# A single-token attention-plus-gMLP block on one core: issuing K and V from the first microsecond, with the weights threaded between heads and one epilogue for both rows

## The chip, the cores and the metric

The kernel runs on one core of one Trainium2 chip. The metric is the device time of one launch in microseconds; medians of several executions are given, and the profile comes from one further execution. The span of the profile is 1.7 us shorter than the device time of the same execution (726.7 against 728.44 us before the change).

Ratios are the mean time of one kernel's fast executions over that of the other's in the same rounds, so they are not quite the ratio of the medians that are quoted.

## The reference, cut to what matters

```python
# B=2 rows, D=512; H=32 heads, Sk=8192 cached keys, Dh=128; F=1792; all bf16
xn = layernorm(x)
q = xn @ wq                                   # wq [512, 4096]
p = softmax(q . k_cache * Dh**-0.5)           # k_cache, v_cache [2, 32, 8192, 128]
attn = (p @ v_cache) @ wo                     # wo [4096, 512]
z = gelu(xn @ w_in)                           # w_in [512, 1792]
z1, z2 = halves(z)
mlp = (z1 * (w_sp * layernorm(z2) + b_sp)) @ w_out   # w_sp and b_sp are one number each
return x + attn + mlp
```

K and V are 268 MB, and each byte is used once. Everything else is 11 MB of weights and some small arithmetic.

## The kernel before

For each of the 64 (row, head) pairs the kernel loads K and V (2 MB each), multiplies K by the broadcast q on VectorE, folds the 128 products of every key by halving adds, lets ScalarE take the exponential, and lets TensorE (PE) form the weighted sum of V. In front stands a prologue: layernorm, q for all heads of both rows, and the whole gMLP. Behind each row stands an epilogue.

```python
pro = pro_stack.enter_context(tc.tile_pool(name="pro", bufs=1))
...
nc.scalar.dma_start(x_rows[:], ...)           # all weights: one block on ScalarE's queue
for c in range(NQC):
    nc.scalar.dma_start(wq_sb[...], ...)
... # x_b, w_sp, b_sp, w_in, w_out, wo, also on nc.scalar
... # layernorm with Ln and Exp; q of both rows; the whole gMLP, ending in hT
pro_stack.close()                             # K and V take over the prologue's memory

kpool = ctx.enter_context(tc.tile_pool(name="kpool", bufs=3))
vpool = ctx.enter_context(tc.tile_pool(name="vpool", bufs=3))
for b in range(B):
    for h in range(H):
        kt = kpool.tile([P, J, Dh], BF16, name="kt")
        nc.sync.dma_start(kt[:], A_k_cache[b, h]...)
        vt = vpool.tile([P, J, Dh], BF16, name="vt")
        nc.sync.dma_start(vt[:], A_v_cache[b, h]...)
        nc.vector.tensor_tensor(out=kt[:], in0=kt[:], in1=q_bcast, op=ALU.mult)
        ... # six halving adds on kt, then the last one into s_t
        nc.scalar.activation(out=e_t[:], in_=s_t[:], func=ACT.Exp, ...)
        ... # 64 matmuls of V by e_t into o_ps[:, h]
    ... # this row's epilogue: l_ps, reciprocal, o_sb, 7 hT and 32 wo matmuls, res, store
```

The scheduler was free to move instructions within an engine's order.

The softmax here doesn't subtract the row's maximum and nothing guards it: scores larger than these inputs give would overflow.

Of the kernel before, what the change touches and what calls it, by code (L numbers as in the profile page):

```python
# [7 lines left out]
BF16 = mybir.dt.bfloat16  # L8
# [6 lines left out]
def kernel(  # L15
# [14 lines left out]
    nc = tc.nc  # L30
# [17 lines left out]
    HPC = NQ // Dh  # L48
# [3 lines left out]
    work = ctx.enter_context(tc.tile_pool(name="work", bufs=2))  # L52
    psum_main = ctx.enter_context(tc.tile_pool(name="psum_main", bufs=1, space=bass.MemoryType.PSUM))
# [5 lines left out]

    x_rows = pro.tile([B, D], BF16, name="x_rows")  # L60
    nc.scalar.dma_start(x_rows[:], A_x.flatten_outer_dims())
    wq_sb = pro.tile([P, KD, HD], BF16, name="wq_sb")
    for c in range(NQC):
        nc.scalar.dma_start(  # L64
            wq_sb[:, :, c * NQ:(c + 1) * NQ],
            A_wq[:, c * NQ:(c + 1) * NQ].rearrange("(k p) n -> p k n", p=P),
        )
    x_b = []
    for b in range(B):
        xb = const.tile([1, D], BF16, name=f"x_b{b}")  # L70
        nc.scalar.dma_start(xb[:], A_x[b])  # L71
        x_b.append(xb)
    wsp_sb = pro.tile([P, 1], BF16, name="wsp_sb")
    nc.scalar.dma_start(wsp_sb[:], B_w_sp[0:1, 0:1].to_broadcast((P, 1)))
    bsp_sb = pro.tile([P, 1], BF16, name="bsp_sb")
    nc.scalar.dma_start(
# [3 lines left out]
    nc.scalar.dma_start(w_in_sb[:], B_w_in.rearrange("(k p) f -> p k f", p=P))  # L80
    w_out_sb = const.tile([P, FC, N_OUT], BF16, name="w_out_sb")
    nc.scalar.dma_start(w_out_sb[:], B_w_out.rearrange("(c p) n -> p c n", p=P))
    wo_sb = const.tile([P, H, N_OUT], BF16, name="wo_sb")
    nc.scalar.dma_start(wo_sb[:], A_wo.rearrange("(h p) n -> p h n", p=P))

    ident = const.tile([B, B], F32, name="ident")
    nc.gpsimd.memset(ident[:], 0.0)
    nc.gpsimd.affine_select(
        out=ident[:],
        in_=ident[:],  # L90
        compare_op=ALU.not_equal,
        fill=1.0,
        base=0,
        pattern=[[-1, B]],
        channel_multiplier=1,
    )
    ones_f = const.tile([P, P], F32, name="ones_f")
    nc.gpsimd.memset(ones_f[:], 1.0)
# [20 lines left out]
    eps_b = pro.tile([B, 1], F32, name="eps_b")  # L119
    nc.vector.memset(eps_b[:], EPS)  # L120
    lnv = pro.tile([B, 1], F32, name="lnv")
    nc.scalar.activation(out=lnv[:], in_=var[:], func=ACT.Ln, bias=eps_b[:], scale=1.0)  # L122
    rstd = pro.tile([B, 1], F32, name="rstd")
    nc.scalar.activation(out=rstd[:], in_=lnv[:], func=ACT.Exp, scale=-0.5)  # L124
# [15 lines left out]
    for b in range(B):  # L140
        for k in range(KD):
            nc.vector.tensor_copy(
                out=xn_rep[:, b, k, :], in_=xnT[:, k, b:b + 1].to_broadcast([P, P])
            )

    qbc = []
    for b in range(B):
        qb = const.tile([P, HD], BF16, name=f"qbc{b}")
        for c in range(NQC):
            q_ps = psum_q.tile([P, NQ], F32, name="q_ps")  # L150
            for k in range(KD):
                nc.tensor.matmul(  # L152
                    q_ps[:], lhsT=xn_rep[:, b, k, :], rhs=wq_sb[:, k, c * NQ:(c + 1) * NQ],
                    start=(k == 0), stop=(k == KD - 1),
                )
            nc.scalar.copy(out=qb[:, c * NQ:(c + 1) * NQ], in_=q_ps[:])  # L156
        qbc.append(qb)

    for c in range(NC2):
        for k in range(KD):  # L160
            nc.tensor.matmul(  # L161
                z_ps[:, c, :], lhsT=w_in_sb[:, k, c * P:(c + 1) * P], rhs=xnT[:, k, :],
                start=(k == 0), stop=(k == KD - 1),
            )
    z_sb = pro.tile([P, NC2, B], F32, name="z_sb")
    nc.vector.tensor_copy(out=z_sb[:], in_=z_ps)  # L166
    zsq = pro.tile([P, NC2, B], F32, name="zsq")
    nc.vector.tensor_tensor(out=zsq[:], in0=z_sb[:], in1=z_sb[:], op=ALU.mult)
    zt = pro.tile([P, NC2, B], F32, name="zt")
    nc.vector.tensor_scalar(out=zt[:], in0=zsq[:], scalar1=0.044715, scalar2=1.0,  # L170
                            op0=ALU.mult, op1=ALU.add)
    nc.vector.tensor_tensor(out=zt[:], in0=zt[:], in1=z_sb[:], op=ALU.mult)
    zexp = pro.tile([P, NC2, B], F32, name="zexp")
    nc.scalar.activation(out=zexp[:], in_=zt[:], func=ACT.Exp, scale=-1.5957691216057308)
    zsig = pro.tile([P, NC2, B], F32, name="zsig")
    nc.vector.tensor_single_scalar(out=zsig[:], in_=zexp[:], scalar=1.0, op=ALU.add)
    nc.vector.reciprocal(out=zsig[:], in_=zsig[:])
    zg = pro.tile([P, NC2, B], F32, name="zg")
    nc.vector.tensor_tensor(out=zg[:], in0=z_sb[:], in1=zsig[:], op=ALU.mult)
    stat = pro.tile([P, 2 * B], F32, name="stat")  # L180
    nc.vector.reduce_sum(
        out=stat[:, 0:B], in_=zg[:, FC:NC2, :].rearrange("p c b -> p b c"),
        axis=mybir.AxisListType.X,
    )
    z2sq = pro.tile([P, FC, B], F32, name="z2sq")
    nc.vector.tensor_tensor(out=z2sq[:], in0=zg[:, FC:NC2, :], in1=zg[:, FC:NC2, :], op=ALU.mult)
    nc.vector.reduce_sum(
        out=stat[:, B:2 * B], in_=z2sq[:].rearrange("p c b -> p b c"),
        axis=mybir.AxisListType.X,
    )  # L190
    nc.tensor.matmul(stat_ps, lhsT=ones_f[:], rhs=stat[:], start=True, stop=True)
    zmean = pro.tile([P, B], F32, name="zmean")
    nc.vector.tensor_single_scalar(out=zmean[:], in_=stat_ps[:, 0:B], scalar=1.0 / Fh, op=ALU.mult)
    zmsq = pro.tile([P, B], F32, name="zmsq")
    nc.vector.tensor_tensor(out=zmsq[:], in0=zmean[:], in1=zmean[:], op=ALU.mult)
    zvar = pro.tile([P, B], F32, name="zvar")
    nc.vector.scalar_tensor_tensor(
        out=zvar[:], in0=stat_ps[:, B:2 * B], scalar=1.0 / Fh, in1=zmsq[:],
        op0=ALU.mult, op1=ALU.subtract,
    )  # L200
    eps_p = pro.tile([P, 1], F32, name="eps_p")
    nc.vector.memset(eps_p[:], EPS)
    zln = pro.tile([P, B], F32, name="zln")
    nc.scalar.activation(out=zln[:], in_=zvar[:], func=ACT.Ln, bias=eps_p[:], scale=1.0)
    zrstd = pro.tile([P, B], F32, name="zrstd")
    nc.scalar.activation(out=zrstd[:], in_=zln[:], func=ACT.Exp, scale=-0.5)  # L206
    wsp_f = pro.tile([P, 1], F32, name="wsp_f")
    nc.vector.tensor_copy(out=wsp_f[:], in_=wsp_sb[:])  # L208
    bsp_f = pro.tile([P, 1], F32, name="bsp_f")
    nc.vector.tensor_copy(out=bsp_f[:], in_=bsp_sb[:])  # L210
    a_t = pro.tile([P, B], F32, name="a_t")
    nc.vector.tensor_single_scalar(out=a_t[:], in_=zrstd[:], scalar=wsp_f[:, 0:1], op=ALU.mult)
    c_t = pro.tile([P, B], F32, name="c_t")
    nc.vector.tensor_tensor(out=c_t[:], in0=zmean[:], in1=a_t[:], op=ALU.mult)
    nc.vector.tensor_scalar(out=c_t[:], in0=c_t[:], scalar1=-1.0, scalar2=bsp_f[:, 0:1],
                            op0=ALU.mult, op1=ALU.add)
    g_t = pro.tile([P, FC, B], F32, name="g_t")
    for b in range(B):
        nc.vector.tensor_scalar(
            out=g_t[:, :, b], in0=zg[:, FC:NC2, b], scalar1=a_t[:, b:b + 1],  # L220
            scalar2=c_t[:, b:b + 1], op0=ALU.mult, op1=ALU.add,
        )
    hT = const.tile([P, FC, B], BF16, name="hT")
    nc.vector.tensor_tensor(out=hT[:], in0=zg[:, 0:FC, :], in1=g_t[:], op=ALU.mult)  # L224
    pro_stack.close()

    kpool = ctx.enter_context(tc.tile_pool(name="kpool", bufs=3))
    vpool = ctx.enter_context(tc.tile_pool(name="vpool", bufs=3))
    spool = ctx.enter_context(tc.tile_pool(name="spool", bufs=3))
    l_all = const.tile([P, B * H], F32, name="l_all")  # L230
    o_sb = const.tile([P, B, H], BF16, name="o_sb")

    for b in range(B):
        o_ps = psum_ob.tile([P, H], F32, name="o_ps")
        for h in range(H):
            gh = b * H + h
            kt = kpool.tile([P, J, Dh], BF16, name="kt")
            nc.sync.dma_start(kt[:], A_k_cache[b, h].rearrange("(p j) d -> p j d", p=P))
            vt = vpool.tile([P, J, Dh], BF16, name="vt")
            nc.sync.dma_start(vt[:], A_v_cache[b, h].rearrange("(p j) d -> p j d", p=P))  # L240
# [18 lines left out]
            for j in range(J):  # L259
# [3 lines left out]
                )  # L263
        l_ps = psum_main.tile([P, H], F32, name="l_ps")
        nc.tensor.matmul(l_ps[:], lhsT=ones_f[:], rhs=l_all[:, b * H:(b + 1) * H],  # L265
                         start=True, stop=True)
        lr = work.tile([P, H], F32, name="lr")
        nc.vector.reciprocal(out=lr[:], in_=l_ps[:])  # L268
        nc.vector.tensor_tensor(out=o_sb[:, b, :], in0=o_ps[:], in1=lr[:], op=ALU.mult)  # L269
# [49 lines left out]
```

## Time and profile before

728.31 us median (726.98 to 730.50, 16 executions). The span of the profile divides as follows. A multiply of K marks the start of each head; "stretch" means from the start of the first multiply to the end of the last head's last add.

| part | us | how it is read |
|---|---|---|
| before the first multiply | 52.9 | timeline |
| 64 heads, 10.21 each | 653.4 | timeline: distance of two multiplies |
| the rest of the stretch, 5.1 of it the stall between the rows | 5.3 | stretch of 658.8 less 653.4 |
| from the last add to the end ("tail") | 14.9 | timeline |
| VectorE busy | 644.2 (89%) | the page's first part |
| DMA while it is backlogged | 423 to 430 GB/s | GB/s row below, slices 5 to 19 |

From the page of the kernel before, second part: the span in 40 equal slices, the busy share of VectorE and of the DMA engines in tenths, and the GB/s moved.

```profile
DVE  1129999999999999999988999999999999999992
...
DMA  9949999999999999999997999999999999999910
GB/s 304 310 180 432 426 427 430 423 427 428 428 428 425 428 428 426 426 430 426 413 419 315 401 408 412 407 411 419 404 411 414 425 395 421 398 413 417 411 80 0
```

VectorE is almost idle in the first three slices (one to two tenths busy) and full afterwards, except in the middle. DMA moves weights in the first two slices and is half idle in the third, before K starts. Both are full in the long stretch. VectorE needs 10.21 us per head; DMA needs 9.8 us, since K and V land 4.90 us apart while there is a backlog. A margin of 4% is not much room. The Trainium skill, "DMA: Bandwidth & Descriptors", section "Specifications", puts the fabric's ceiling at 435 GB/s; the trace's 423 to 430 lies just below it.

The timeline of the kernel before, start to first multiply. Columns: start in us, duration in us, engine and line, operation, output<-inputs, count, and in brackets the idle time of the engine and what ended it. ACT is ScalarE, DVE is VectorE, SPq is SyncE's queue of DMA issues.

```profile
16.04 1.28 ACT L122 ACT_TABLE_LOAD   x1 [16.04 <-DMA bsp_sb<-in_B_b_sp_dram]
...
19.17 0.53 DVE L126 TENSOR_SCALAR xn_rows<-x_f,mean,rstd 2x512 f32<-2x512 f32 x1 [2.88 <-ACT rstd L124]
...
38.30 0.19 DVE L166 COPY z_sb<-zst_ps 128x28 f32<-128x28 f32 x1 [16.48 <-PE zst_ps L161]
...
44.85 0.17 DVE L224 TENSOR_TENSOR hT<-zg,g_t 128x14 bf16<-128x14 f32 x1
...
45.15 0.36 SPq L238 DMA_DIRECT2D kt<-in_A_k_cache_dram  x1
...
52.93 4.43 DVE L242 TENSOR_TENSOR kt<-kt,qbc 128x8192 bf16<-128x8192 bf16 x1 [7.91 <-DMA kt<-in_A_k_cache_dram]
```

ScalarE issued the weights until 16.0 us and only then began the layernorm's logarithm, though VectorE had its input ready at 4.25. (The first line names the landing of b_sp, which fell at the same moment; the logarithm does not read it.) The prologue ended with hT at 45.0 us, and K was issued right then: the waits of SyncE's queue (us in total, times, longest) name hT as what it waited for last.

```profile
SPq L238 <- DVE hT L224: 24.2, 1, 24.2
```

K does not need hT as data: it waited for the prologue's memory to come free.

The row boundary of the kernel before, VectorE's part of the timeline:

```profile
382.68 0.36 DVE L268 RECIPROCAL lr<-l_ps 128x32 f32<-128x32 f32 x1 [2.85 <-PE l_ps L265]
...
383.19 4.42 DVE L242 TENSOR_TENSOR kt<-kt,qbc 128x8192 bf16<-128x8192 bf16 x1
...
392.34 0.68 DVE L287 TENSOR_TENSOR res<-out_ps,x_b 1x512 bf16<-1x512 f32 x1 [1.15 <-PE out_ps L281]
...
395.10 4.42 DVE L242 TENSOR_TENSOR kt<-kt,qbc 128x8192 bf16<-128x8192 bf16 x1
...
405.31 4.42 DVE L242 TENSOR_TENSOR kt<-kt,qbc 128x8192 bf16<-128x8192 bf16 x1
```

The last two lines stand the usual 10.21 us apart. VectorE waited 2.85 us for PE's sums and 1.15 us for the first row's output. The multiply of the head before had started at 369.54, so two distances are long here, 13.65 and 11.91 us instead of 10.21, 5.1 us in sum. The tail of the kernel before, PE's part:

```profile
712.22 1.85 PE L260 MATMUL o_ps<-e_t,vt 128*128 128x1 bf16 x64 [8.37 <-ACT e_t L255]
713.93 0.61 PE L265 MATMUL l_ps<-l_all,ones_f 128*128 128x32 f32 x2
715.22 8.58 PE L281 MATMUL out_ps<-wo_sb,o_sb 128*1 128x512 bf16 x32 [0.68 <-DVE o_sb L269]
```

### The profile page before, as it was taken

Reading aid. Unit: us, or ns where it says so; the run is one execution under the profiler, and the core shown is the slowest. Engines: PE = TensorE matmul, PEld = TensorE weight load, DVE = VectorE, ACT = ScalarE, POOL = GpSimd, SP = SyncE. Lnnn points to the kernel's source line nnn. Section 1 sums busy time; section 2 is a strip of 40 time slices with the busy share of each in tenths; the row PEclk is TensorE's granted clock in tenths of the full one; section 3 lists DMA queues with packets and bytes.
Section 4 is the critical chain, followed back from the end, with each engine's and each line's share of the span. In section 5 each row is a group of like instructions: output and inputs, shape, how many; then the busy total and the mean of one; then the engine's idle time right before and its main releaser. Section 6 shows DMA issues by size and latency. Waiting matters only on the chain.

```text
span 726.7 us, 9772 instructions
## 1 busy us (share of the span) xinstructions
PE 159.7 (22%) x4304; PEld 132.0 (18%) x4304; DVE 644.2 (89%) x558; ACT 38.4 (5%) x153; POOL 0.6 (0%) x7
## 2 busy tenths in 40 slices
PE   0831222122211222122217112221122212221126
PEld 0411221111111111011113111111111101111112
DVE  1129999999999999999988999999999999999992
ACT  1520000000000000000000000000000000000000
POOL 0000000000000000000000000000000000000000
PEclk9965555555555555555557555555555555555557
DMA  9949999999999999999997999999999999999910
GB/s 304 310 180 432 426 427 430 423 427 428 428 428 425 428 428 426 426 430 426 413 419 315 401 408 412 407 411 419 404 411 414 425 395 421 398 413 417 411 80 0
DMA packets 28550, 280.21 MB, mean 386 GB/s; under 512 B 2518, under 2 KB 11612, under 8 KB 12124
## 3 DMA queue, kind: packets, MB, share of 16 engines
q1 hardware_dynamic: 18432, 268.44, 88.6%
q10 hardware_dynamic: 10076, 11.15, 4.7%
q8 instruction: 33, 0.54, 0.3%
q14 instruction: 9, 0.07, 0.0%
HBM read 279.58 MB, written 0.00 MB: 385 GB/s over the span
## 4 chain that ended last, share of the span: by engine, by line
DVE 86%; PE 6%; DMA 3%; issue 2%; ACTq 1%; ACT 1%; DVEq 0%; SPq 0%
DVE kt L246 46%; DVE kt L242 37%; DVE s_t L251 3%; PE out_ps L281 2%; DMA kt<-in_A_k_cache_dram 2%; PE q_ps L152 2%; ACTq L64 1%; DMA bsp_sb<-in_B_b_sp_dram 1%; PE o_ps L260 1%; ACTq L71 0%; PE zst_ps L161 0%; DVE res L287 0%; ACT L206 0%; ACT L124 0%; ACT L122 0%
## 5 line engine op out<-in xcount | busy, mean ns | idle before, releaser
L246 DVE TENSOR_TENSOR kt<-kt 128x4096 bf16<-128x4096 bf16 (+5 forms) x384 | 337.0, 878 | 13.1
L242 DVE TENSOR_TENSOR kt<-kt,qbc 128x8192 bf16<-128x8192 bf16 x64 | 282.8, 4419 | 8.1 <-DMA kt<-in_A_k_cache_dram 8.1
L260 PE MATMUL o_ps<-e_t,vt 128*128 128x1 bf16 x4096 | 118.0, 165 | 535.3 <-ACT e_t L255 535.3
L260 PEld LDWEIGHTS <-vt 128*128 128x128 bf16 x4096 | 114.9, 104 | 539.6 <-issue 526.0
L255 ACT ACTIVATE e_t<-s_t 128x64 bf16<-128x64 f32 x64 | 16.5, 258 | 645.8 <-DVE s_t L251 645.8
L251 DVE TENSOR_TENSOR s_t<-kt 128x64 f32<-128x64 bf16 x64 | 19.3, 301 | 6.4
L281 PE MATMUL out_ps<-wo_sb,o_sb 128*1 128x512 bf16 x64 | 17.6, 443 | 1.4 <-DVE o_sb L269 1.4
L152 PE MATMUL q_ps<-wq_sb,xn_rep 128*128 128x512 bf16 x64 | 16.0, 416 | 0.0
L166 DVE COPY z_sb<-zst_ps 128x28 f32<-128x28 f32 x1 | 0.2, 187 | 16.5 <-PE zst_ps L161 16.5
L255 ACT ACTIVATION_READ_ACCUMULATOR e_t<-s_t 128x1 f32 x64 | 12.1, 188 | 0.1
L208 DVE CAST wsp_f<-wsp_sb 128x1 f32<-128x1 bf16 x1 | 0.2, 154 | 11.7 <-DMA wsp_sb<-in_B_w_sp_dram 11.7
L287 DVE TENSOR_TENSOR res<-out_ps,x_b 1x512 bf16<-1x512 f32 x2 | 1.4, 678 | 9.8 <-PE out_ps L281 9.8
L156 ACT CAST qbc<-q_ps 128x512 bf16<-128x512 f32 x16 | 9.4, 587 | 9.4 <-PE q_ps L152 9.4
L152 PEld LDWEIGHTS <-xn_rep 128*128 128x128 bf16 x64 | 6.7, 106 | 8.8 <-issue 2.1
L281 PEld LDWEIGHTS <-o_sb 128*1 128x1 bf16 x64 | 5.9, 94 | 12.3 <-issue 5.0
L275 PE MATMUL out_ps<-w_out_sb,hT 128*1 128x512 bf16 x14 | 4.8, 501 | 4.7 <-DVE hT L224 3.9
L268 DVE RECIPROCAL lr<-l_ps 128x32 f32<-128x32 f32 x2 | 0.7, 358 | 5.7 <-PE l_ps L265 5.7
L136 PE MATMUL zst_ps<-ident,xn_rows 2*128 2x2 f32 x4 | 0.6, 240 | 19.9 <-DVE xn_rows L126 19.9
L136 PEld LDWEIGHTS zst_ps<-ident,xn_rows 2*128 2x128 f32 x4 | 0.5, 209 | 19.8 <-issue 19.8
L126 DVE TENSOR_SCALAR xn_rows<-x_f,mean,rstd 2x512 f32<-2x512 f32 x1 | 0.5, 532 | 2.9 <-ACT rstd L124 2.9
L275 PEld LDWEIGHTS <-hT 128*1 128x1 bf16 x14 | 1.3, 98 | 7.4 <-DVE hT L224 4.0
L122 ACT ACT_TABLE_LOAD x1 | 1.3, 1283 | 16.0 <-DMA bsp_sb<-in_B_b_sp_dram 16.0
(51 smaller groups left out, 20.0 us busy)
## 6 DMA issues: line engine op xcount, KB each, us to landing
kt<-in_A_k_cache_dram SPq DMA_DIRECT2D x64, 2048.0 KB, 10.4
vt<-in_A_v_cache_dram SPq DMA_DIRECT2D x64, 2048.0 KB, 13.4
wq_sb<-in_A_wq_dram ACTq DMA_DIRECT2D x8, 512.0 KB, 7.9
wo_sb<-in_A_wo_dram ACTq DMA_DIRECT2D x1, 4096.0 KB, 21.4
w_in_sb<-in_B_w_in_dram ACTq DMA_DIRECT2D x1, 1792.0 KB, 9.9
w_out_sb<-in_B_w_out_dram ACTq DMA_DIRECT2D x1, 896.0 KB, 11.0
x_b<-in_A_x_dram ACTq DMA_DIRECT2D x2, 1.0 KB
out_dram<-res ACTq DMA_DIRECT2D x2, 1.0 KB
```

Source lines behind the costliest of these rows:

```text
L64: nc.scalar.dma_start(wq_sb[:, :, c * NQ:(c + 1) * NQ], A_wq[:, c * NQ:(c + 1) * NQ].rearrange("(k p) n -> p k n", p=P),)
L122: nc.scalar.activation(out=lnv[:], in_=var[:], func=ACT.Ln, bias=eps_b[:], scale=1.0)
L152: nc.tensor.matmul(q_ps[:], lhsT=xn_rep[:, b, k, :], rhs=wq_sb[:, k, c * NQ:(c + 1) * NQ], start=(k == 0), stop=(k == KD - 1),)
L156: nc.scalar.copy(out=qb[:, c * NQ:(c + 1) * NQ], in_=q_ps[:])
L242: nc.vector.tensor_tensor(out=kt[:], in0=kt[:], in1=q_bcast, op=ALU.mult)
L246: nc.vector.tensor_tensor(out=kt[:, :, 0:hw], in0=kt[:, :, 0:hw], in1=kt[:, :, hw:w], op=ALU.add)
L251: nc.vector.tensor_tensor(out=s_t[:].unsqueeze(2), in0=kt[:, :, 0:1], in1=kt[:, :, 1:2], op=ALU.add)
L255: nc.scalar.activation(out=e_t[:], in_=s_t[:], func=ACT.Exp, scale=SCALE, accum_out=l_all[:, gh:gh + 1],)
L260: nc.tensor.matmul(o_ps[:, h:h + 1], lhsT=vt[:, j, :], rhs=e_t[:, j:j + 1], start=(j == 0), stop=(j == J - 1),)
L275: nc.tensor.matmul(out_ps[:], lhsT=hT[:, c, b:b + 1], rhs=w_out_sb[:, c, :], start=(idx == 0), stop=(idx == n_mm - 1),)
L281: nc.tensor.matmul(out_ps[:], lhsT=o_sb[:, b, h:h + 1], rhs=wo_sb[:, h, :], start=(idx == 0), stop=(idx == n_mm - 1),)
L287: nc.vector.tensor_tensor(out=res[:], in0=out_ps[:], in1=x_b[b][:], op=ALU.add)
```

## The change

The intent: start K and V at once instead of after the prologue, let the prologue's work ride in gaps between heads, and pay for one epilogue instead of two. The diff, cut to its core:

```diff
+    kpool, vpool, spool opened first: K and V have their own memory; V bufs 3 -> 2
+    ctx.enter_context(tc.manual_schedule(engines={DVE, PE, Activation, SP}))  # order as written
-    nc.scalar.dma_start(...)                 # all weights up front
+    nc.sync.dma_start(x_rows[:], ...)        # x, wq chunk 0, then K0, K1, V0, ...
+    issue_wq(0)
+    nc.gpsimd.dma_start(wsp_sb[:], ...)      # the two scalars, from GpSimd
+    nc.gpsimd.dma_start(bsp_sb[:], ...)
-    activation(Ln); activation(Exp, scale=-0.5)
+    activation(Sqrt); vector.reciprocal
+    make_rep(0); make_q(0, 0)                # q for the first four heads only
+    def issue_kv(b, h): ...                  # K runs one head ahead of V in the queue
+    def loads(b, h):                         # weights behind head h's K and V
+        if b == 0 and h % 4 == 1: issue_wq(h // 4 + 1)
+        if b == 1: w_in at h == 2; w_out at h == 10; one of 8 chunks of wo at h == 12, 14, ... 26
+    def small(b, h):                         # small work behind head h
+        if b == 0 and h % 4 == 2: make_q(0, h // 4 + 1)
+        if b == 0 and h == 12: make_rep(1)
+        if b == 0 and h >= 24: make_q(1, h - 24)
+        if b == 1 and 5 <= h <= 9: next(gm)  # the gMLP in five pieces
-    two epilogues with [1, 512] outputs
+    # one epilogue: 7 hT matmuls, l_ps for both rows, reciprocal, o_sb, 32 wo matmuls, res
```

## The prediction

> **What bounds the kernel now.** VectorE: 97% busy from 60 to 380 and from 400 to 700 us (windowed table). In the timeline a multiply starts every 10.21 us, so 64 heads are 653.4 us of the 726.7 us span. The rest:
> - the first multiply starts at 52.93 us; no K is issued before 45.15, which waited for hT, the prologue's last result (queue waits);
> - between the rows a stall of 5.1 us (15.35 us between the K issues at 379.86 and 395.21);
> - 15.0 us from the last add (711.72) to the end.
>
> DMA is nearly as loaded. While backlogged, transfers of K or V land 4.90 us apart (428 GB/s), so 9.8 us per head. Weights are 11.15 MB; wq chunks (0.5 MB) land 1.51 us apart.
>
> **What changes.** K and V start right behind x and the first wq chunk; the other weights ride between heads on the same queue; q is made by chunks; the gMLP is cut into pieces behind heads 5 to 9 of row 1; one epilogue serves both rows; V has two buffers, not three.
>
> Terms, in us:
> 1. Start: -42.2. q for the first heads is ready near 9.4 (VectorE chain to var at 4.2 as now, then square root, normalise, transposes, replication, four cold matmuls of 0.43, copy 0.59); K0 lands near 10.7 behind wq chunk 0.
> 2. Row-boundary stall gone: -5.1.
> 3. VectorE pays inside the loop for gMLP and the second row's replication, until now before the first K: +5.2 (timeline durations with gaps).
> 4. Epilogue: +1.7. The seven hT matmuls, done mid-kernel until now, follow the last head in PE's order, ahead of the sums: +3.0 (0.43 each). They should warm the clock: in the old tail it went full 6.2 us after PE began, and the last 24 of 32 wo matmuls took 0.22. All 32 warm: -1.6. The Trainium skill, "TensorE: Matmul & The Clock Gate", Part 1, gives a free-running activity window for this; the trace agrees in kind (0.43 to 0.22) but waits longer than the page's 3.4 us.
>
> Span: 10.7 + 653.4 + 5.2 + 16.7 = 686. The measured time is 1.7 over the span: **688 us**.
>
> **Does DMA keep up?** A weight load delays K and V whichever engine issues it (the skill, "DMA: Bandwidth & Descriptors", "Issuing engines are not separate DMA queues"). An estimate, first in first out with these durations: K lands about 5 us before its multiply throughout row 0 (each wq chunk eats what four heads gain), and 1 to 2 us before it near head 60. V is sometimes late for PE, which VectorE does not feel. So no stall, but no room: at 5.0 per transfer VectorE would lose about 7 us, at 5.1 about 19. The third V buffer changes nothing here.
>
> Range 683 to 700. Faster by over 2%: 0.96; within: 0.035; slower: 0.005.
>
> **What would show each step.** First multiply at 10 to 12 us; spacing 10.21 across the boundary; VectorE delays of 1 to 2 us behind heads 6 to 9 of row 1, little idle until K elsewhere; 428 GB/s nearly throughout; 16 to 18.5 us from last add to end, wo matmuls near 0.22.
>
> **What would make it wrong.** Slow transfers: from 340 us on, the trace shows packets of up to 2.7 us and 400 to 420 GB/s. I take that for queues that run empty; if it is the second row's data, K comes late and the time is 695 to 705. Or wo rows of 1 KB cost more among 16 KB packets, or a cold tail.

## The result, and the profile after

691.86 us median (690.09 to 693.19, 8 executions), against 728.31 before; ratio 0.9497, 95% interval 0.9486 to 0.9509: 5% faster. The profiled execution took 689.93 us, the fastest of the nine, with a span of 688.2.

| part, us | before | predicted | profile after |
|---|---|---|---|
| first multiply starts at | 52.93 | 10.7 | 12.62 |
| stretch, first multiply to last add | 658.8 | 658.6 | 658.8 |
| tail | 14.9 | 16.7 | 16.8 |
| span | 726.7 | 686 | 688.2 |

The page after, second part, with PEclk, PE's granted clock in tenths:

```profile
DVE  4999999999999999999999999999999999999991
...
PEclk9999999999999999999999999999999999999999
DMA  7999999999999999999999999999999999999960
GB/s 315 423 429 425 419 430 417 428 422 428 428 417 430 415 430 425 423 429 428 429 426 420 429 426 425 425 419 421 420 422 425 423 419 420 420 425 423 427 286 1
```

VectorE and DMA are full from the first slices to the last but one or two. Do not lean on this PEclk row: it says full clock throughout, but the kernel's own 512-column matmuls took 0.43 us up to the tail, twice what they take at full clock, and the trace holds no clock record before 676 us. The Trainium skill, "TensorE: Matmul & The Clock Gate", section "Seeing it yourself", warns that clock events in traces have been seen to be unreliable. This row fits the warning: where no record exists, it shows full clock, and that is plainly wrong here.

The timeline after, lines from the start:

```profile
4.31 1.28 ACT L133 ACT_TABLE_LOAD   x1 [4.31 <-DVE var L128]
...
9.80 0.59 ACT L168 CAST qbc<-q_ps 128x512 bf16<-128x512 f32 x1 [3.90 <-PE q_ps L164]
...
12.62 4.42 DVE L293 TENSOR_TENSOR kt<-kt,qbc 128x8192 bf16<-128x8192 bf16 x1 [4.39 <-DMA kt<-in_A_k_cache_dram]
```

q was ready at 10.39 us (9.80 + 0.59); the first multiply still waited until 12.62 for K0. The waits for K later on, from the same timeline (VectorE in row 1):

```profile
588.28 4.42 DVE L293 TENSOR_TENSOR kt<-kt,qbc 128x8192 bf16<-128x8192 bf16 x1 [0.56 <-DMA kt<-in_A_k_cache_dram]
...
609.37 4.43 DVE L293 TENSOR_TENSOR kt<-kt,qbc 128x8192 bf16<-128x8192 bf16 x1 [0.57 <-DMA kt<-in_A_k_cache_dram]
...
630.45 4.42 DVE L293 TENSOR_TENSOR kt<-kt,qbc 128x8192 bf16<-128x8192 bf16 x1 [0.57 <-DMA kt<-in_A_k_cache_dram]
```

At three heads, and by 0.1 us at one before them, K came late: multiplies stood 10.35, 10.86, 10.87 and 10.86 us apart instead of 10.21, that is 2.1 us in sum. At the boundary between the rows nothing is left to see; the first multiply of row 1 follows its neighbour in 10.21 us:

```profile
338.75 4.42 DVE L293 TENSOR_TENSOR kt<-kt,qbc 128x8192 bf16<-128x8192 bf16 x1
...
348.96 4.42 DVE L293 TENSOR_TENSOR kt<-kt,qbc 128x8192 bf16<-128x8192 bf16 x1
```

The tail after, PE and VectorE:

```profile
673.66 3.03 PE L319 MATMUL out_ps<-w_out_sb,hT 128*2 128x512 bf16 x7
...
676.62 0.43 PE L324 MATMUL l_ps<-l_all,ones_f 128*128 128x64 f32 x2
...
678.03 7.07 PE L331 MATMUL out_ps<-wo_sb,o_sb 128*2 128x512 bf16 x32 [0.97 <-DVE o_sb L328]
```

The seven hT matmuls now stand between the last PV and the sums (3.0 us), and all 32 wo matmuls then run at 0.22 us.

### The profile page after: what moved, and what is told of

It is laid out like the page before. It is cut to its first block, busy times and chain, and to the rows that moved or that the text cites. A ratio compares the mean times of both kernels' runs of the same rounds, so it can differ in the third digit from the quotient of the medians.

```text
span 688.2 us, 9628 instructions
## 1 busy us (share of the span) xinstructions
PE 159.7 (23%) x4263; PEld 127.8 (19%) x4263; DVE 643.3 (93%) x556; ACT 37.8 (5%) x151; POOL 1.9 (0%) x10
## 4 chain that ended last, share of the span: by engine, by line
DVE 88%; DMA 8%; issue 2%; PE 2%; DVEq 0%; SPq 0%; ACT 0%; ACTq 0%
DVE kt L297 46%; DVE kt L293 38%; DMA kt<-in_A_k_cache_dram 8%; DVE s_t L302 2%; PE out_ps L331 1%; PE out_ps L319 0%; PE o_ps L311 0%; DVEq L302 0%; DVE res L336 0%; DVE lr L326 0%; DVE xn_rep L154 0%; DVE g_t L241 0%; SPq L68 0%; PE l_ps L324 0%; SPq L64 0%
## 5 line engine op out<-in xcount | busy, mean ns | idle before, releaser
L306 ACT ACTIVATE e_t<-s_t 128x64 bf16<-128x64 f32 x64 | 16.5, 258 | 553.5 <-DVE s_t L302 522.7
L164 PE MATMUL q_ps<-wq_sb,xn_rep 128*128 128x512 bf16 x64 | 29.7, 623 | 0.5 <-DVE xn_rep L154 0.5
L331 PE MATMUL out_ps<-wo_sb,o_sb 128*2 128x512 bf16 x32 | 7.1, 379 | 1.0 <-DVE o_sb L328 1.0
L331 PEld LDWEIGHTS <-o_sb 128*2 128x2 bf16 x32 | 2.6, 85 | 5.0 <-DVE o_sb L328 1.1
L306 ACT ACT_TABLE_LOAD x2 | 2.6, 1283 | 8.6 <-DVE wsp_f L229 8.6
L319 PE MATMUL out_ps<-w_out_sb,hT 128*2 128x512 bf16 x7 | 3.0, 608 | 0.0
L176 PE MATMUL zst_ps<-xnT,w_in_sb 128*128 128x2 bf16 x56 | 1.6, 165 | 0.0
L176 PEld LDWEIGHTS <-w_in_sb 128*128 128x128 bf16 x56 | 1.6, 104 | 0.0
## 6 DMA issues: line engine op xcount, KB each, us to landing
kt<-in_A_k_cache_dram SPq DMA_DIRECT2D x64, 2048.0 KB, 16.7
```

What stands on the lines that cost most here:

```text
L164: nc.tensor.matmul(q_ps[:], lhsT=xn_rep[:, b, k, :], rhs=wq_sb[:, k, c * NQ:(c + 1) * NQ], start=(k == 0), stop=(k == KD - 1),)
L176: nc.tensor.matmul(z_ps[:, c, :], lhsT=w_in_sb[:, k, c * P:(c + 1) * P], rhs=xnT[:, k, :], start=(k == 0), stop=(k == KD - 1),)
L306: nc.scalar.activation(out=e_t[:], in_=s_t[:], func=ACT.Exp, scale=SCALE, accum_out=l_all[:, gh:gh + 1],)
L319: nc.tensor.matmul(out_ps[:], lhsT=hT[:, c, :], rhs=w_out_sb[:, c, :], start=(c == 0), stop=False,)
L331: nc.tensor.matmul(out_ps[:], lhsT=o_sb[:, :, h], rhs=wo_sb[:, h, :], start=False, stop=(h == H - 1),)
```

## The experiments

Theories. Mine: VectorE (10.21 us per head plus small work) and DMA (all bytes, one queue) are both within about 1% of setting the pace of the stretch; whatever delays VectorE early gives DMA time, and whatever loads DMA late shows as waits for K. The rival: VectorE alone sets it, and costs simply add. Side questions: why K0 came 1.9 us later than predicted, whether two V buffers cost anything, what the tail depends on, and whether the wait for memory alone explains the 40 us at the start.

The stretch, first multiply to last add, is read from each profile; it leaves the tail out, which varies by itself as will be seen. "Late K" is the sum by which multiplies at run heads 54 to 60 (counted from 0) stood further apart than 10.21 us. "Cold" counts the wo matmuls at 0.43 us among the 32.

| run | median us (executions) | ratio to before | first multiply | stretch | late K | tail | cold |
|---|---|---|---|---|---|---|---|
| before | 728.31 (16) | 1 | 52.93 | 658.8 | none | 14.9 | 7 |
| after | 691.86 (8) | 0.9497 | 12.62 | 658.8 | 2.1 | 16.8 | 0 |
| after_again | 691.95 (5) | 0.9482 | 12.74 | 658.6 | 2.0 | 17.1 | 0 |
| a_bcast_late | 689.57 (4) | 0.9460 | 10.53 | 658.9 | 2.3 | 17.0 | 0 |
| b_hT_early | 688.66 (4) | 0.9451 | 11.68 | 659.2 | 2.5 | 15.4 | 7 |
| c_dve_plus | 690.76 (4) | 0.9475 | 11.72 | 659.1 | none | 18.7 | 8 |
| d_wo_late | 689.27 (5) | 0.9449 | 11.65 | 656.6 | none | 19.4 | 11 |
| cd_dve_plus_wo_late | 690.36 (5) | 0.9467 | 11.85 | 659.1 | none | 18.6 | 7 |
| v3_buffers | 691.69 (4) | 0.9477 | 11.78 | 659.2 | 2.6 | 16.9 | 0 |
| f_norm_per_row | 691.81 (4) | 0.9488 | 11.77 | 661.8 | none | 16.4 | 3 |
| h_warm | 688.53 (4) | 0.9437 | 11.82 | 659.2 | 2.5 | 16.5 | 14 |
| e_before_pools2 | 725.29 (6) | 0.9946 | 45.73 | 662.7 | - | 15.4 | 10 |
| g_all | 683.97 (5) | 0.9376 | 9.17 | 657.4 | none | 15.6 | 9 |
| g2_warm_full | 682.55 (4) | 0.9364 | 9.09 | 657.4 | none | 13.9 | 0 |

All gave correct results. The runs were made in three groups, each on its own chip; the interval of each ratio is about 0.002 to either side, so differences of 1 to 2 us between runs rest on the profiles rather than on the medians.

### Control: the changed kernel again

> The changed kernel itself, as the control on the chip and in the rounds of the runs beside it. 690 to 693 us; first multiply at 11.5 to 12.7 us, late K waits of about 2 us in sum at heads 54 to 60 of the run, and a tail of 16.8 to 19.4 us, according to how many of the 32 wo matmuls (0 to 11 in the runs so far) run at 0.43 us before the clock goes full.

As expected: 691.95 us, the late waits, and a tail within the range.

### Where the start went: the two scalars not loaded by GpSimd

```diff
-    nc.gpsimd.dma_start(wsp_sb[:], ...); nc.gpsimd.dma_start(bsp_sb[:], ...)
+        if b == 1 and h == 2: nc.sync.dma_start(wsp_sb[:], ...); nc.sync.dma_start(bsp_sb[:], ...)
```

> The changed kernel, but the two scalars of the gMLP are no longer loaded by GpSimd at the start; SyncE loads them in row 1, head 2. In the changed kernel the DMA engines were only 6 to 10 of 16 busy from 5.0 to 8.5 us, just when GpSimd's 2-byte packets ran (5.2 to 10.9 us), and K0 landed at 12.5 us instead of the predicted 10.7. Theory 1 (those small loads disturb the start): no dip, first multiply at 10.6 to 11.0 us, the whole 1.5 to 2 us shorter, because the DMA time that was lost comes back at the end too. Theory 2 (the dip is the start of large transfers on a cold queue): first multiply stays at 12.4 to 12.8, time unchanged within 0.5 us.

The table by stretches of one microsecond; columns: window, length, busy us and instruction count of PE, PEld, DVE, ACT and POOL, clock, busy share of the DMA engines, GB/s. The changed kernel first, then this run.

```profile
5.00:6.00 1.00, 0.00 (x0) 0.00 (x0) 0.07 (x1) 0.88 (x2) 0.00 (x0) 1.00 0.33 115
6.00:7.00 1.00, 0.20 (x2) 0.23 (x3) 0.61 (x2) 0.00 (x0) 0.00 (x0) 1.00 0.37 147
7.00:8.00 1.00, 0.48 (x5) 0.37 (x4) 0.58 (x4) 0.00 (x0) 0.00 (x0) 1.00 0.70 279
```

```profile
5.00:6.00 1.00, 0.00 (x0) 0.00 (x0) 0.04 (x1) 0.92 (x2) 0.00 (x0) 1.00 1.07 442
6.00:7.00 1.00, 0.17 (x2) 0.20 (x3) 0.65 (x2) 0.00 (x0) 0.00 (x0) 1.00 0.86 360
7.00:8.00 1.00, 0.48 (x5) 0.40 (x4) 0.54 (x4) 0.00 (x0) 0.00 (x0) 1.00 1.08 459
```

With the scalars loaded by GpSimd, DMA moved 115, 147 and 279 GB/s in these three microseconds, just while GpSimd's packets ran (5.2 to 10.9 us in the trace); without them 442, 360 and 459. K0 landed at 10.4 us instead of 12.5, the first multiply started at 10.53, and the last add ended 1.9 us earlier (669.46 against 671.39). Removing the GpSimd loads removed the dip: theory 1 holds. By what mechanism loads of 512 bytes in all hold up the others was not tried. Nor is it shown why K0 came 0.8 to 1.1 us later in the changed kernel and its control than in the other runs with a dip of that size. The dip cost 1.6 to 1.8 us of all 16 engines' time in every run that kept these loads (the idle share summed from 3 to 12 us), and 0.1 us here.

That the gain survived to the end is telling. Among the runs with the dip, the first multiply came at 11.7 to 11.8 in some and at 12.6 to 12.7 in others. Of those that change nothing else in the stretch's work, the early ones (b_hT_early, v3_buffers, h_warm) ended the last add at 670.9 to 671.0, the late ones (the changed kernel and its control) at 671.3 to 671.4: a start 0.8 to 1.1 us earlier was worth 0.3 to 0.5 us. In this one run the DMA time won back was worth about its full length (the last add came 1.4 to 1.9 us earlier than in those five); an earlier VectorE alone mostly waits more for K later.

### Are VectorE and DMA both at the limit? Three runs

Useless VectorE work in row 0:

```diff
+        if b == 0 and h == 16:
+            for i in range(2):   # overwritten later by q of row 1
+                nc.vector.tensor_tensor(out=qbc[1][:, i*2048:(i+1)*2048],
+                    in0=qbc[0][:, 0:2048], in1=qbc[0][:, 0:2048], op=ALU.mult)
```

> The changed kernel with 2.45 us of useless VectorE work (two products of 128x2048, overwritten later) behind head 16 of row 0. Theory 1 (VectorE and DMA are both at their limit, and late in row 1 VectorE waits 2.1 us for K): the extra work gives the DMA time to get ahead, the waits at heads 54 to 60 vanish, and the whole is only 0.2 to 0.8 us longer. Theory 2 (VectorE alone sets the time, the terms just add): 2.3 to 2.6 us longer.

Four of the eight wo chunks moved to the end of the queue:

```diff
-        if 12 <= h <= 26 and h % 2 == 0: one chunk
+        if 12 <= h <= 18 and h % 2 == 0: one chunk
+        if h == H - 1: chunks 4, 5, 6, 7
```

> The changed kernel, but the last four of the eight wo chunks (2 MB) are issued behind the last V instead of between heads 20 and 26 of row 1. Theory 1 (the K waits of 2.1 us at heads 54 to 60 come from these chunks pushing K back on a saturated DMA): the waits vanish, the chunks land near 676 us, before the wo matmuls, and the whole is 1.7 to 2.3 us shorter. Theory 2 (the waits have another cause, such as V buffers that come free late): the waits stay and the whole is unchanged within 0.5 us, or longer if the chunks come too late for the tail.

Both edits:

> Both earlier edits at once: 2.45 us of useless VectorE work in row 0, and the last four wo chunks behind the last V. With the extra work alone the stretch from first multiply to last add grew by 0.3 us; with the chunks moved alone it shrank by 2.2 us. Theory 1 (with the chunks out of the way only VectorE sets the pace): the extra work now costs its full 2.2 to 2.4 us: 658.7 to 659.1 us for the stretch, against 656.6 with the chunks moved alone. Theory 2 (extra work is always hidden): 656.6 to 657.2.

VectorE's waits for K in the three kernels (who waited for whom: us in total, times, longest): the changed kernel, then c_dve_plus, then d_wo_late. Each total contains the one wait for K0 at the start, the "longest".

```profile
DVE kt L293 <- DMA kt<-in_A_k_cache_dram: 6.1, 4, 4.4
```

```profile
DVE kt L298 <- DMA kt<-in_A_k_cache_dram: 3.5, 1, 3.5
```

```profile
DVE kt L297 <- DMA kt<-in_A_k_cache_dram: 3.2, 1, 3.2
```

In both edits only the wait at the start is left. Compared with the three kernels that start at the same time and leave this part alone (b_hT_early, v3_buffers, h_warm: 659.2 us each), the extra work, which held up one head by 2.2 us (12.41 us between multiplies), left the stretch as it was (659.1; 0.3 us more than the changed kernel, which starts later), since the late waits for K vanished. Moving the chunks shortened the stretch by 2.6 us (2.2 against the changed kernel). With the chunks out of the way the same extra work cost 2.45 us (659.06 against 656.61). So the extra work is free only while late chunks make K the limit: theory 1 in all three. The chunks landed by 668.7 us (676 was expected), before the wo matmuls needed them.

The medians would have misled here: d_wo_late has the shortest stretch of the first four runs, but its profile has the longest tail, 19.4 us, because 11 of its wo matmuls were cold:

```profile
675.27 9.35 PE L335 MATMUL out_ps<-wo_sb,o_sb 128*2 128x512 bf16 x32 [0.97 <-DVE o_sb L332]
```

### Undoing the single epilogue in part: row 0 normalised at the boundary

```diff
+        # at the end of each row: l_ps, reciprocal, o_sb for this row
-    # for both rows at the end
```

> The changed kernel with row 0's sums, reciprocal and scaling back at the row boundary, as in the kernel before; the wo matmuls stay at the end. VectorE then waits at the boundary again, 3.3 to 3.5 us. Theory 1 (DMA catches up during it): the K waits at heads 54 to 60 vanish, so from first multiply to last add only 1.2 to 1.8 us more than the control's 658.6 to 659.2. Theory 2 (terms add): 3.3 us more.

The stretch was 661.8 us, 3.1 us over the changed kernel and 2.6 over v3_buffers, its neighbour with the same start. That lies between the two theories, because the stall itself was larger than expected. The timeline at the boundary:

```profile
340.63 1.49 PE L164 MATMUL q_ps<-wq_sb,xn_rep 128*128 128x512 bf16 x3 [0.24 <-issue]
...
342.42 0.36 DVE L320 RECIPROCAL lr<-l_ps 128x32 f32<-128x32 f32 x1 [4.43 <-PE l_ps L317]
```

VectorE waited 4.43 us for the sums: in PE's fixed order the q matmuls behind head 31 (1.5 us) came first, and V had been late. The multiplies at the boundary stood 15.22 us apart, a stall of 5.0 us, of which about half was given back by the late K waits, which vanished (2.6 us in v3_buffers). This supports the give-back, but my size for the stall was wrong. The medians of the two (0.9488 and 0.9477) don't tell them apart.

### Do two V buffers cost anything?

```diff
-    vpool bufs=2
+    vpool bufs=3    # room from normalising x in place and a bf16 scratch
```

> The changed kernel with three V buffers instead of two (room made by normalising x in place and by a bf16 scratch that nobody reads). Theory 1 (the prediction's: DMA and VectorE set the time, PE's waits for V cost nothing): V is issued earlier, but K lands no earlier, K waits of 1.5 to 2.2 us in row 1 stay, whole unchanged within 1 us of the control (688.4 us span with a tail of 16.8 to 19.4). Theory 2 (the late K waits come from V buffers that come free late and hold up the queue): waits gone, 2 us shorter.

```profile
DVE kt L293 <- DMA kt<-in_A_k_cache_dram: 5.7, 5, 3.4
```

The waits for K stayed, the one of 3.4 us for K0 and four late ones: stretch 659.2, late K 2.6 us. The late waits don't come from V buffers, and PE's long waits for V (360 us in sum in the changed kernel) cost nothing.

### The tail: hT matmuls earlier, and warming matmuls

```diff
+        if b == 1 and h == 16: the seven hT matmuls      # instead of behind the last head
```

> The changed kernel, but the seven hT matmuls are written behind head 16 of row 1 instead of behind the last head. Theory 1 (they lie on the tail's chain, and they also warm the clock): the tail from last add to end, 16.8 us, loses 3.0 but the first 8 or so of 32 wo matmuls run at 0.43 again, so 15.2 to 15.5 us, and the whole is 1.2 to 1.7 us shorter. Theory 2 (the clock is warm anyway by then): the tail is 13.8 us and the whole 3 us shorter. If they cost nothing where they are: no change.

The tail was 15.4 us, with seven cold matmuls: theory 1 for the profiled executions. The medians fell by more than the 1.2 to 1.7 us expected, by some 2 to 3 us (0.9451 against 0.9482 and 0.9497, with about 2 us of noise); whether that is more than noise is not shown.

```diff
+        if b == 1 and 28 <= h <= 30: 16 matmuls of 512 columns whose result nobody reads
```

> The hT matmuls behind head 16 of row 1, as in the run before, and 16 useless 512-column matmuls behind each of heads 28, 29 and 30 of row 1, while PE would wait for VectorE, to keep PE busy before the tail. Theory 1 (a cold clock at the start of the tail is what costs there): the clock is full when the tail begins, all 32 wo matmuls take 0.22, the tail from last add to end is 13.3 to 14.2 us, and the whole is 3 to 5 us shorter than the control. Theory 2 (PE is not warmed by such spurts, or the last PV is delayed by them): the tail stays at 15 us or more.

The expectation failed: 14 cold matmuls and a tail of 16.5 us. The clock went back and forth, full for 3.4 or 6.8 us and half for as long, and fell to half at 673.5 us, 1 us before the wo matmuls began. By stretches (same columns as above):

```profile
659.90:666.70 6.80, 3.88 (x74) 2.49 (x74) 6.63 (x5) 0.35 (x2) 0.00 (x0) 1.00 0.75 318
666.70:670.10 3.40, 3.40 (x10) 1.22 (x8) 3.26 (x5) 0.00 (x0) 0.00 (x0) 0.50 0.23 92
670.10:673.50 3.40, 3.13 (x71) 2.27 (x69) 0.74 (x3) 0.35 (x2) 0.00 (x0) 1.00 0.00 0
673.50:680.30 6.80, 5.84 (x14) 1.74 (x15) 0.84 (x3) 0.00 (x0) 0.00 (x0) 0.50 0.00 0
```

Idle time of PE alone does not explain this: in the third piece PE was busy for 3.13 of 3.40 us, mostly with one-column matmuls, and half clock followed. A count over the clock records of all fourteen profiles says more. The stretches of one clock in the records last multiples of 3.41 us; cut into pieces of that length, they show that what counted was how many matmuls of 512 columns ran in the piece before a change. At half clock, full clock followed all 22 pieces with more than 6.1 of them, none of 1556 with fewer than 5.5 (parts of matmuls counted), and 2 of the 6 between. At full clock it stayed after all 51 pieces with 6.7 or more and fell after all 34 with 5.3 or fewer. So the limit here lies near six, and one-column matmuls did not make up for missing ones: in d_wo_late PE was busy all through 669.67 to 673.08, with 6.1 of them, and the clock stayed at half. In h_warm the piece from 670.1 to 673.5 held 4.5. At full clock the 16 warming matmuls of a head are through sooner, and the piece behind them holds too few.

The median (0.9437 against 0.9482 for the control beside it) is shorter all the same. That fits that the hT matmuls no longer stand in the tail, since b_hT_early had 0.9451 without any warming; the medians say nothing for or against the warming.

### Does the wait for memory alone explain the start?

This is the kernel before with one edit.

```diff
+    kpool, vpool (bufs 2), spool opened ahead of the prologue's pools; those closed at the end
```

> The kernel before, with the K, V and score pools opened ahead of the prologue's pool (and V cut to two buffers, so that all fits), nothing else: K and V need not wait for hT's memory any more, while weights stay on ScalarE's queue in one block and the scheduler stays automatic. Theory 1 (the early start needs q early too, so the weights must be cut and interleaved): K lands early, but w_in and all of wq share the DMA engines with five K and V buffers, and PE's order has gMLP matmuls ahead of q; first multiply at 30 to 45 us, and the whole 8 to 22 us shorter than before (706 to 720). Theory 2 (the wait for the memory alone was the cost): first multiply near 12 to 15 us, whole 690 to 695.

It gained less than either theory said: 725.29 us, ratio 0.9946, interval 0.9932 to 0.9959. The timeline, of SyncE's queue, ScalarE, PE and VectorE:

```profile
0.73 0.37 SPq L236 DMA_DIRECT2D kt<-in_A_k_cache_dram  x1
```

```profile
30.81 1.29 ACTq L87 DMA_DIRECT2D wo_sb<-in_A_wo_dram  x1
32.13 1.28 ACT L125 ACT_TABLE_LOAD   x1 [32.13 <-issue]
...
45.11 0.58 ACT L159 CAST qbc<-q_ps 128x512 bf16<-128x512 f32 x1 [9.87 <-PE q_ps L155]
```

```profile
42.73 0.62 PE L164 MATMUL zst_ps<-xnT,w_in_sb 128*128 128x2 bf16 x17 [6.22 <-DMA w_in_sb<-in_B_w_in_dram]
```

```profile
45.73 8.76 DVE L240 TENSOR_TENSOR kt<-kt,qbc 128x8192 bf16<-128x8192 bf16 x2 [7.81 <-ACT qbc L159]
```

K0 was issued at 0.73 us. But now K and V kept the DMA engines busy from the start, the weights on ScalarE's queue came slower, ScalarE went on issuing them until 32.1 us instead of 16.0, and only then came to the layernorm's logarithm, whose input had been there since 4.25. Then PE, in whose order the first gMLP matmuls stand before q's, waited 6.2 us more for w_in. q for the first heads was ready at 45.7, against 23.8 in the kernel before. After that, VectorE waited 3.3 us for K at two early heads, so the stretch grew by 3.9 us. So the other parts of the change, q by chunks, weights behind K and V, and issuing taken off ScalarE, carry most of the gain at the start, 40.3 us in the changed kernel against 7.2 us here. Which of them carries how much was not separated.

### A version that beats both

g_all combines the late scalars, the early hT matmuls, the warming matmuls, the last four wo chunks behind the last V, a dummy Sqrt at the start (so that its table load does not wait for the data), and K0 loaded and multiplied in two halves. The dummy Sqrt and the halves were not tried alone.

> A version meant to beat both: scalars loaded late, hT matmuls early, warming matmuls, the last four wo chunks behind the last V, Sqrt's table brought early by a dummy Sqrt, and K0 loaded and multiplied in two halves. Sum of the parts: first multiply at 9.1 to 10.5 us (q ready 1.3 earlier), no K waits, VectorE loop 653.4 + 3.5 for small work, tail 13.3 to 14.2: span 679 to 682, that is 681 to 684 us, 8 to 10 us under the control. If DMA is still the limit, K waits come back and it gains less than 6.

g2_warm_full is the same with the warming enlarged:

```diff
-        if b == 1 and 28 <= h <= 30: 16 warming matmuls
+        if b == 1 and 25 <= h <= 30: 32 warming matmuls
```

> The best version so far, with 32 useless matmuls behind each of heads 57 to 62 of the run counted in row 1 (25 to 30) instead of 16 behind three of them. With 16 the granted clock alternated between full and half, since about 4 us of each head stayed idle, and 9 of the 32 wo matmuls of the tail were cold. Theory 1 (PE must be busy nearly all the time to stay at full clock): now 0 to 2 are cold, the tail is 13.3 to 14.2 us instead of 15.6, the whole 681.5 to 683. Theory 2: tail unchanged near 15.5, or the last PV is late because a cold batch takes 13.8 us, and the whole is longer.

g_all took 683.97 us, ratio 0.9376; g2_warm_full 682.55, ratio 0.9364, interval 0.9346 to 0.9382, against 0.9477 for v3_buffers and 0.9488 for f_norm_per_row in the same rounds. The first multiply came at 9.1 to 9.2 us, and the stretch shrank to 657.4. VectorE still waited 0.6 to 0.7 us for K at head 36, two heads behind the load of w_in. g_all's tail of 15.6 us missed the 13.3 to 14.2 expected, with nine cold matmuls. In g2_warm_full, with PE kept busy, no wo matmul was cold:

```profile
667.59 1.74 PE L337 MATMUL o_ps<-e_t,vt 128*128 128x1 bf16 x64
...
670.58 7.07 PE L351 MATMUL out_ps<-wo_sb,o_sb 128*2 128x512 bf16 x32 [0.97 <-DVE o_sb L348]
```

The tail was 13.9 us. The last PV began at 667.59, 1.1 us behind the last add instead of 0.5, since a warming batch was still running; fewer warming matmuls were not tried. The intervals of the two versions overlap, so only the profiles say that the second is the better one.

## Why the prediction was right

- **Faster by 5%, inside the range.** 691.86 us against 688 (683 to 700). The profiled span was 2.2 us over the sum.
- **Start, -42.2 predicted, -40.3 measured.** The mechanism was right. The step that was off is "K0 lands near 10.7 behind wq chunk 0": it landed at 12.5 (11.5 to 11.8 in most later runs), because of the scalars' loads by GpSimd, whose disturbance I had not counted; without them it was 10.4. q came 1.0 us later than predicted, at 10.39: I had the Sqrt's table loaded early, but the load stood behind the wait for its data (4.31 to 5.59). The wait for K0 hid that.
- **Boundary stall gone, -5.1.** Right: 10.21 us across the boundary.
- **VectorE's small work, +5.2.** The stretch exceeded 64 heads by 5.3 us, but not from that term alone. The small work delayed heads by 4.3 us in sum (0.5 behind head 12 of row 0; 0.8, 1.2, 0.4 and 1.5 behind heads 6 to 9 of row 1). Eighteen heads took 10.14 or 10.15 us instead of 10.21, 1.2 us less, for which no run gives the reason. And K was late by 2.1 us. These happen to add up.
- **"So no stall, but no room."** Nearly: "1 to 2 us before it near head 60" became up to 0.6 us late. VectorE ran some 2 us faster than in my sum, and that time came off K's margin. The runs confirm the rest: DMA at its limit, the chunks of wo as the cause, and a third V buffer without effect.
- **Tail, +1.7.** 16.8 us against 16.7, but the profile met the best case. The 3.0 us of hT matmuls stand as predicted; whether the clock is full by the wo matmuls depends on how the 3.41 us pieces of the clock happen to lie over the hT matmuls, and that differs between executions: in the changed kernel one piece (673.03 to 676.44) held 6.5 of the seven, while in c_dve_plus they were split, 2.7 and 4.3. Seven profiles of kernels that keep the tail in this form, the changed kernel and its control among them, show 0 to 11 cold matmuls and 16.8 to 19.4 us. That the executions without a profile were mostly slower than the profiled one (690.1 to 693.2 against 689.9) fits such cold tails, but was not shown.
- **What I had listed as dangers.** Transfers in row 1 were not slow: 419 to 429 GB/s in slices 21 to 38. So the second row's data did not cause the 395 to 425 GB/s of the kernel before in its second half. Their mean over slices 23 to 38 is 410, and 4.19 MB of K and V per 10.21 us are 411: DMA had caught up there and moved at VectorE's pace.

## What to carry to other kernels

When two resources are within a few per cent of each other, costs don't add: delay on one is given back by the other, and a saving on one turns into a wait for the other, so read which wait ends last at the end of the stretch, and order the loads by when they are needed (what only the epilogue needs goes behind the last K). An early start needs the whole chain early: memory freed alone gained 0.5%, while the layernorm sat behind ScalarE's own DMA issues and q's matmuls behind PE's wait for w_in. Compare parts of a few microseconds in the profile, stage by stage, since a tail of PE work varies by 2 to 3 us with the phase of its clock.

## What the Trainium skill lacked or had wrong

- "DMA: Bandwidth & Descriptors": lacks that small loads issued by GpSimd can hold up the large loads of SyncE. Here two loads of 128 two-byte elements went with 1.6 to 1.8 us of lost DMA time and K0 1.1 to 2.2 us later. Its section "Issuing engines are not separate DMA queues" says that issuing from several engines saves only the sequencer's time; e_before_pools2 agrees that they share: ScalarE was issuing weights until 32.1 us instead of 16.0 once K and V ran beside them. I found no sentence there that warns that the issuing engine's own computing waits behind its issues; here the layernorm's logarithm began with the last issue's end, at 16.0 us in the kernel before and at 32.1 in e_before_pools2.
- "TensorE: Matmul & The Clock Gate", Part 1: a window of 3.4 us. The trace agrees with the unit (full and half clock in pieces of 3.4 and 6.8 us in h_warm). I found no sentence there on how much work makes a window count as busy: here about six matmuls of 512 columns in 3.41 us (full clock after every piece with more than 6.1, after none with fewer than 5.5), while one-column matmuls did not help. So full clock came 4.6 to 11.2 us after the start of the last PV, by how the pieces lay over the seven hT matmuls and the pause of about 1 us behind them.
- "ScalarE: Activation LUTs", section "What ACT_TABLE_LOAD costs": about 1283 ns for the load agrees (1.28 us here). The further 1380 ns of draining did not show: the Sqrt began at 5.60 us, right where its load from 4.31 ended. In the kernel before, the load for the exponential started at 17.64, 0.02 us after the logarithm, and the exponential began at 18.94, 0.02 us after its load.
- No page has that a trace's clock may read full for a whole kernel whose matmuls run at half, beyond the general warning quoted above; here it did in the changed kernel's profile, where the clock's records begin at 676 us.
